# First-batch theta as float32 products, with the weights' two-part split moved beside the second attention

## The chip, the cores and the metric

The kernel runs on one core of a Trainium2 chip. The metric is the device time of one execution in microseconds. Three runs of the kernel before gave 557.42, 557.12 and 552.5 us, median 557.12 us. The profiled execution took 554.9 us, of which the span from the first to the last instruction is 553.1 us.

## The reference

The computation is a chain of three blocks over 4 batches of 576 positions with 512 channels.

- Windowed attention with 8 heads of 64 channels. Each position sees at most 32 keys, plain neighbours in heads 0 to 3 and every fourth position in heads 4 to 7. The result x has shape (4, 576, 512).
- A mixing block: theta = x @ w_theta, zr = x cos(theta), zi = x sin(theta), y = w_tok_r zr + w_tok_i zi over the positions, u = x + y, and x2 = u + relu(u @ w_ch).
- A gated block: h = relu(x2 @ w_in), its second half normalised and mixed over positions with w_spatial and b_spatial, multiplied with the first half, times w_out.

The weights arrive as float64 and are turned to float32 on the chip.

## The kernel before, in words

**Products in parts.** Outside the attention a float32 product is made of three products of type float32r (F32R): an operand a is split into a rounded part ah and a rest al, and a @ b is ah bh + al bh + ah bl. Three instructions per contraction block of 128, so twelve per tile where the contraction is 512. The attention's own products, and the transposes, are plain float32 (F32) instructions of TensorE (L252, L280, L294, L298, L372). A score product (L252) fills one half of the output's rows; two successive ones fill the two halves.

**Weights from float64.** `bits64` (L116) loads a piece of a weight, scales its high words on an engine (L130 on ScalarE or L132 on GpSimd) and puts the bits together in three VectorE instructions (L133 to L135) by way of one PSUM tile, c64. `split_weight` (L138) then copies the rounded part (L108, L110 or L112, by engine) and subtracts it for the rest (L146, GpSimd or VectorE). For w_theta (`w_theta_job`, L161, eight jobs: four blocks k of 128 rows, two halves c of 256 columns) copy and subtraction are both on GpSimd. The jobs are put between the score steps of the first batch's attention (L512 to L515), each tied behind the softmax of a step. Their loads stand in SP's queue ahead of those of w_tok.

**Theta.** `th_unit(b, t)` (L339) works on 128 positions (t = 0 to 3), or on the last 64 (t = 4). It scales x by 1/(2 pi) into the rounded part h (L352 on ScalarE in batch 0, L354 on VectorE later), makes the rest l (L355, VectorE), and issues the twelve products into one PSUM tile (L360). The result, in turns, is reduced to its fraction (L368 on ScalarE, L369 on VectorE), x is transposed on TensorE (L372), sine and cosine come from ScalarE (L377, L378, and L374 for the absolute value), VectorE multiplies them with the transposed x (L381, L388, L389), and the two results are split into zh (L110, L112 or L108) and zl (L332 on GpSimd).

**Order of the work.** Each engine works through its instructions in order. The program sets that order from generators that are run side by side (`spread`, L471, with rates), and a planner with its own estimate of times arranges what it emits. The first batch runs attention(0) with the w_theta jobs, then th_run(0) in the order t = 4, 0, 1, 2, 3 with the first half of w_tok beside it (L522), then tm_run(0) (the products with w_tok, L431 and L438) with attention(1) and the job list `j_tok1 + j_ch` beside it (L525 to L527), where j_ch are the four w_ch jobs. th_run(1) comes after (L528). Loads for the heads of attention(1) are tied behind the last load of the first half of w_tok (L234).

**Buffers.** ps_mm has 4 PSUM tiles, used by scores, theta and the w_tok products. The `stage` tiles of `bits64` are 4, the tiles xh and xl of theta 2 each.

Of the kernel before, what the change touches and what calls it, by code (L numbers as in the profile page):

```python
# [11 lines left out]
F32 = mybir.dt.float32  # L12
F32R = mybir.dt.float32r
BF16 = mybir.dt.bfloat16
U32 = mybir.dt.uint32
AF = mybir.ActivationFunctionType
ALU = mybir.AluOpType
# [5 lines left out]
DM = H * D  # L23
P = 128
# [12 lines left out]
INV2PI = float(np.float32(1.0 / (2.0 * math.pi)))  # L37
# [15 lines left out]
IN_ENG, SP_ENG, OUT_ENG = "vgg", "ag", "aga"  # L53
TOK_ENG = ("aga", "gv")
CH_ENG = "vga"
THETA_ENG = "gg"
Z_HI = ("v", "g")

K_MAIN = (0, 4, 1, 5, 2, 6, 3, 7)
# [4 lines left out]
def tile_block(ctx: ExitStack, tc: tile.TileContext, qT, kT, vw, eye_in, mask_in, eye_b_in, w_theta, w_tok, w_ch, w_in, w_sp, w_sph, b_sp, w_out, out):  # L64
    nc = tc.nc
    V, A, G, PE, SY = nc.vector, nc.scalar, nc.gpsimd, nc.tensor, nc.sync

    def f32(ap):
        return ap.bitcast(F32)
# [3 lines left out]
    ps_mm = ctx.enter_context(tc.tile_pool(name="ps_mm", bufs=4, space=PSUM))  # L73
# [18 lines left out]
    pz = tc.alloc_tile_pool(name="pz", bufs=1, side="left")  # L92
# [3 lines left out]
    pth = tc.alloc_tile_pool(name="pth", bufs=1, side="right")  # L96
    wth_h = pth.tile([P, 4, DM], F32R, name="wth_h")
    wth_l = pth.tile([P, 4, DM], F32R, name="wth_l")
# [7 lines left out]
    def copy(dst, src, eng):  # L106
        if eng == "a":
            A.copy(dst, src)  # L108
        elif eng == "v":
            V.tensor_copy(dst, src)  # L110
        else:
            G.tensor_scalar(dst, src, 1.0, 1.0, op0=ALU.mult, op1=ALU.mult)  # L112
# [3 lines left out]
    def bits64(src, n, eng, st=None):  # L116

        p = src.shape[0]  # L120
        if st is None:
            st = const.tile([P, 2 * CH], U32, tag="w64", name="w64", bufs=4)
        last_dma[0] = SY.dma_start(st[:p, :2 * n], src.bitcast(U32))
        w = st[:p, :2 * n].rearrange("p (n w) -> p n w", w=2)
        lw, hw = w[:, :, 0], w[:, :, 1]
        g = const.tile([P, CH], F32, tag="stage", name="w64g", bufs=4)[:p, :n]
        c = c64[:p, :n].bitcast(U32)
        gi = g.bitcast(U32)
        if eng == "a":
            A.mul(g, hw.bitcast(F32), 2.0**-112)  # L130
        else:
            G.tensor_scalar(g, hw.bitcast(F32), 2.0**-56, 2.0**-56, op0=ALU.mult, op1=ALU.mult)  # L132
        V.tensor_scalar(c, lw, 29, None, op0=ALU.logical_shift_right)  # L133
        V.scalar_tensor_tensor(c, gi, 3, c, op0=ALU.logical_shift_left, op1=ALU.bitwise_or)
        V.scalar_tensor_tensor(gi, gi, 0x80000000, c, op0=ALU.bitwise_and, op1=ALU.bitwise_or)  # L135
        return g

    def split_weight(src, hi, lo, eng_hi, eng_lo, eng_bits="g", st=None):  # L138
        n = hi.shape[-1]
        if src.dtype == F32:  # L140
            s = const.tile([P, CH], F32, tag="stage", name="stage", bufs=4)[:src.shape[0], :n]
            SY.dma_start(s, src)
        else:
            s = bits64(src, n, eng_bits, st)
        copy(hi, s, eng_hi)
        (G if eng_lo == "g" else V).tensor_tensor(lo, s, f32(hi), op=ALU.subtract)  # L146

    def halves(src, hi, lo, k, n, engs):

        for c in range(2):  # L150
            cs = slice(n // 2 * c, n // 2 * (c + 1))
            split_weight(src[:, k, cs], hi[:, k, cs], lo[:, k, cs], *engs)

    def stored(src, dst, k, cs, engs):
# [3 lines left out]
        split_weight(src[:, k, cs], t[:, 0], t[:, 1], *engs)  # L158
        SY.dma_start(f32(dst[:, k, :, cs]), f32(t))

    def w_theta_job(k, c):  # L161
        cs = slice(DM // 2 * c, DM // 2 * (c + 1))
        split_weight(w_theta[:, k, cs], wth_h[:, k, cs], wth_l[:, k, cs], *THETA_ENG, st=pz.tile([P, DM], U32, tag=f"z{'hl'[c]}{k}", name="wth64"))

    def w_tok_job(k, c):
        cs = slice(CH * c, CH * (c + 1))
# [4 lines left out]
    def w_ch_job(k):  # L171
        if not wch:
            wch.extend(p1.tile([P, 4, DM], F32R, tag=n, name=n) for n in ("wch_h", "wch_l"))
        halves(w_ch, *wch, k, DM, CH_ENG)
# [155 lines left out]
    def split(dst_h, dst_l, src, eh="a", el="g"):  # L330
        copy(dst_h, src, eh)
        return (G if el == "g" else V).tensor_tensor(dst_l, src, f32(dst_h), op=ALU.subtract)  # L332

    def ztile(k, bufs=1):
        h = pz.tile([P, DM], F32R, tag=f"zh{k}", name=f"zh{k}", bufs=bufs)
        l = pz.tile([P, DM], F32R, tag=f"zl{k}", name=f"zl{k}", bufs=bufs)
        return h, l

    def th_unit(b, t, pair=False):  # L339


        n = P if pair or t < 4 else HALF
        if pair:
            src = xs[b]
            V.tensor_copy(src[:, :, HALF:], x[b + 1][:, :, 4 * P:])
        else:
            src = x[b][:, :, P * t:P * t + n]
        h = pth.tile([P, 4, P], F32R, tag="xh", name="xh", bufs=2)[:, :, :n]
        l = pth.tile([P, 4, P], F32R, tag="xl", name="xl", bufs=2)[:, :, :n]

        if b == 0:
            A.mul(h, src, INV2PI)  # L352
        else:
            V.tensor_scalar(h, src, INV2PI, None, op0=ALU.mult)  # L354
        V.scalar_tensor_tensor(l, src, INV2PI, f32(h), op0=ALU.mult, op1=ALU.subtract)  # L355
        ps = ps_mm.tile([P, 512], F32, tag="mm", name="ps_th")[:n]
        i = 0
        for k in range(4):
            for lh, rh in ((h, wth_h), (l, wth_h), (h, wth_l)):
                PE.matmul(ps, lh[:, k, :], rh[:, k, :], start=(i == 0), stop=(i == 11))  # L360
                i += 1
        if b == 0 and t in (0, 1):
            if not t:
                spare.append(p1.tile([P, 4, DM], F32, tag="uh", name="spare"))
            ta, tb = (spare[0][:, 2 * t + i, :] for i in range(2))
        else:
            ta, tb = (pth.tile([P, DM], F32, tag=g, name=g, bufs=2)[:n] for g in ("ta", "tb"))
        A.activation(ta, ps, AF.Identity, bias=magic[:n, 0:1])  # L368
        V.scalar_tensor_tensor(ta, ta, MAGIC, ps, op0=ALU.subtract, op1=ALU.subtract)  # L369
        xn = ps_t.tile([P, 512], F32, tag="pt", name="ps_xn")[:n]  # L370
        for k in range(4):
            turned[b, t] = PE.transpose(xn[:, P * k:P * (k + 1)], src[:, k, :], ident)  # L372
        if b == 0:
            A.activation(tb, ta, AF.Abs)  # L374
        else:
            V.tensor_scalar(tb.bitcast(U32), ta.bitcast(U32), 0x7FFFFFFF, None, op0=ALU.bitwise_and)
        A.activation(ta, ta, AF.Sin, scale=-TURN)  # L377
        ia = A.activation(tb, tb, AF.Sin, scale=-TURN, bias=half_pi[:n, 0:1])  # L378
        if t < 4:
            for k, tt in ((t, tb), (4 + t, ta)):  # L380
                iv = V.tensor_tensor(tt, xn, tt, op=ALU.mult)  # L381
                zh[b, k], zl[b, k] = ztile(k)
                zlast[b] = ia, iv, split(zh[b, k], zl[b, k], tt, Z_HI[k // 4], "g")
        else:
            for i in range(2 if pair else 1):
                r_ = slice(HALF * i, HALF * (i + 1))
                zz = pth.tile([P, DM], F32, tag=("ta", "tb")[i], name="zz", bufs=2)
                V.tensor_tensor(zz[:HALF], xn[r_], tb[r_], op=ALU.mult)  # L388
                V.tensor_tensor(zz[HALF:], xn[r_], ta[r_], op=ALU.mult)  # L389
                zh[b + i, 8], zl[b + i, 8] = ztile(8, 2)  # L390
                split(zh[b + i, 8], zl[b + i, 8], zz, "a", "g")
# [9 lines left out]
    def th_shared(b):  # L401
        th_unit(b, 4, True)
        yield

    def th_run(b, ts):
        for t in ts:
            th_unit(b, t)
            yield
# [84 lines left out]
        for g in gens:  # L493
            yield from g

    j_ch = [lambda k=k: w_ch_job(k) for k in range(4)]

    H2 = DM // 2
    j_in = [lambda k=k, c=c: stored(w_in, win_d, k, slice(H2 * c, H2 * (c + 1)), IN_ENG) for c in (2, 3, 0, 1) for k in range(4)]
# [12 lines left out]
    for m, _ in enumerate(attention(0)):  # L512
        for i in range(8):
            if m == TH_FROM + TH_RATE * i // 10:
                behind(softmax[m], lambda: w_theta_job(i // 2, i % 2))  # L515
# [49 lines left out]
    for hf in (1, 0):  # L565
        cs = slice(DM * hf, DM * (hf + 1))
# [3 lines left out]
    n = 0  # L570
# [61 lines left out]
    gg = {}  # L632
# [212 lines left out]
```

## Time and profile before

| what | value |
|---|---|
| runs (us) | 557.42, 557.12, 552.5 |
| median | 557.12 us |
| profiled execution | 554.9 us |
| its span | 553.1 us, 11234 instructions |
| busy: TensorE products, weight loads | 531.0 us, 474.5 us |
| busy: VectorE, ScalarE, GpSimd | 320.3, 244.2, 262.9 us |
| mean granted TensorE clock | 0.997 of full speed |

Times are microseconds from the start of the span. PE is TensorE's products, PEld its weight loads, DVE is VectorE, ACT ScalarE, POOL GpSimd, SP the queue that issues most transfers. A product's recorded duration has the way through the array in it; how fast products follow each other is read from the starts.

### The profile page before, as it was taken

To read this page: it belongs to the slowest core of one execution; us is meant where nothing else is said; L and a number is where in the kernel's file an instruction comes from. 1 tells how busy PE (TensorE), PEld (TensorE's weight loads), DVE (VectorE), ACT (ScalarE), POOL (GpSimd) and SP (SyncE) were. 2 spreads that over 40 slices of the span, in tenths; PEclk is the share of its full clock that TensorE was granted. 3 is DMA by queue.
4 is the path that set the end of the run, shared out by engine and by line. 5 is a ranking of instruction groups with operands and counts; after the bars stand their busy time and mean duration, and the time that the engine had idled before them with its cause. 6 is when DMAs were issued, how large, how long until landed. Compare 5 with 4: busy or idle time off the path is not lost.

```text
span 553.1 us, 11234 instructions
## 1 busy us (share of the span) xinstructions
PE 531.0 (96%) x4148; PEld 474.5 (86%) x4148; DVE 320.3 (58%) x835; ACT 244.2 (44%) x717; POOL 262.9 (48%) x333
## 2 busy tenths in 40 slices
PE   5997999999999999988999999999999999999997
PEld 3665888989889989877889999899899889988996
DVE  2698998898787487632694139862702148253020
ACT  3869765635656254663452114542322233233221
POOL 3494994645984359641188336363202204322040
PEclk9999999999999999998999999999999999999999
DMA  8925766660588353770005978848015110002002
GB/s 203 300 93 156 191 180 189 182 198 35 162 235 232 95 175 120 230 228 25 1 1 155 370 250 286 265 131 289 20 58 172 58 38 1 1 1 77 0 1 96
DMA packets 50223, 76.07 MB, mean 138 GB/s; under 512 B 4084, under 2 KB 30968, under 8 KB 50168
## 3 DMA queue, kind: packets, MB, share of 16 engines
q1 hardware_dynamic: 49944, 75.17, 44.3%
q8 instruction: 33, 0.54, 0.4%
q10 hardware_dynamic: 224, 0.18, 0.1%
q14 instruction: 22, 0.18, 0.1%
HBM read 52.53 MB, written 22.81 MB: 136 GB/s over the span
## 4 chain that ended last, share of the span: by engine, by line
PE 52%; DMA 3%; POOL 1%; ACT 1%; issue 1%; DVE 1%; SPq 0%; ACTq 0%; POOLq 0%; DVEq 0%
PE ps_sp L719 9%; PE ps_hu L700 9%; PE ps_o L748 9%; PE ps_hv L655 9%; PE ps_y L438 7%; PE ps_r L457 4%; PE ps_th L360 1%; DMA wsp_d<-parts 1%; DMA win_d<-parts 1%; PE ps_sp L722 1%; PE ps_sp L721 1%; POOL zl L332 0%; POOL parts L146 0%; ACT parts L108 0%; DVE ta L381 0%
## 5 line engine op out<-in xcount | busy, mean ns | idle before, releaser
L438 PE MATMUL ps_y<-wtok_h,zh 128*128 128x288 f32 x270 | 82.1, 308 | 0.7 <-DVE sm L263 0.4
L438 PE MATMUL ps_y<-wtok_h,zl 128*128 128x288 f32 x270 | 81.0, 301 | 0.4 <-POOL zl L332 0.4
L438 PE MATMUL ps_y<-wtok_l,zh 128*128 128x288 f32 x270 | 79.8, 299 | 0.0
L332 POOL TENSOR_TENSOR gl<-hu,gh 128x288 fp32r<-128x288 f32 x32 | 26.0, 813 | 71.4 <-ACT gh L108 71.4
L438 PEld LDWEIGHTS ps_y<-wtok_h,zh 128*128 128x128 f32 x270 | 50.7, 189 | 3.2 <-DVE sm L263 0.9
L438 PEld LDWEIGHTS ps_y<-wtok_h,zl 128*128 128x128 f32 x270 | 51.2, 189 | 1.7 <-POOL zl L332 0.8
L723 DVE TENSOR_TENSOR hu<-ps_sp,hu 128x288 f32<-128x288 f32 x32 | 14.6, 456 | 63.5 <-PE ps_sp L722 63.5
L438 PEld LDWEIGHTS ps_y<-wtok_l,zh 128*128 128x128 f32 x270 | 50.7, 189 | 0.6
L332 POOL TENSOR_TENSOR vl<-hv,vh 128x512 fp32r<-128x512 f32 x16 | 20.9, 1308 | 58.1 <-ACT vh L108 53.1
L270 POOL TENSOR_TENSOR sm<-sm,l 128x288 f32<-128x288 f32 x48 | 32.0, 672 | 27.6 <-DVE l L269 14.7
L267 ACT ACTIVATE sm<-sm,m 128x96 f32<-128x96 f32 x108 | 39.2, 364 | 12.8 <-DVE m L264 6.7
L332 POOL TENSOR_TENSOR ul<-x,uh 128x288 fp32r<-128x288 f32 x32 | 26.7, 841 | 26.4 <-ACT uh L108 26.1
L719 PE MATMUL ps_sp<-wsp_h,vh 128*128 128x288 f32 x128 | 37.8, 295 | 0.0
L457 PE MATMUL ps_r<-uh,wch_h 128*128 128x288 f32 x128 | 37.6, 300 | 0.2 <-DVE x L441 0.2
L719 PE MATMUL ps_sp<-wsp_l,vh 128*128 128x288 f32 x128 | 37.8, 295 | 0.0
L719 PE MATMUL ps_sp<-wsp_h,vl 128*128 128x288 f32 x128 | 37.8, 295 | 0.0
L700 PE MATMUL ps_hu<-x2h,win_h 128*128 128x288 f32 x128 | 37.7, 294 | 0.0
L700 PE MATMUL ps_hu<-x2h,win_l 128*128 128x288 f32 x128 | 37.7, 294 | 0.0
L700 PE MATMUL ps_hu<-x2l,win_h 128*128 128x288 f32 x128 | 37.7, 294 | 0.0
L457 PE MATMUL ps_r<-uh,wch_l 128*128 128x288 f32 x128 | 37.5, 296 | 0.0
L441 DVE TENSOR_TENSOR x<-ps_y,x 128x288 f32<-128x288 f32 x40 | 17.6, 448 | 33.9 <-PE ps_y L438 33.8
L457 PE MATMUL ps_r<-ul,wch_h 128*128 128x288 f32 x128 | 36.7, 295 | 0.0
(182 smaller groups left out, 1577.7 us busy)
## 6 DMA issues: line engine op xcount, KB each, us to landing
x2d<-parts SPq DMA_DIRECT2D x32, 288.0 KB, 2.7
vt<-vw SPq DMA_DIRECT2D x16, 432.0 KB, 4.6
w<-w_tok SPq DMA_DIRECT2D x18, 288.0 KB, 4.7
x2h<-x2d SPq DMA_DIRECT2D x8, 576.0 KB, 7.8
x2l<-x2d SPq DMA_DIRECT2D x8, 576.0 KB, 8.3
kt<-kT SPq DMA_DIRECT2D x15, 304.0 KB, 4.2
w<-w_in SPq DMA_DIRECT2D x16, 256.0 KB, 3.3
win_d<-parts SPq DMA_DIRECT2D x16, 256.0 KB, 2.5
```

The lines of the kernel that those rows point to most:

```text
L267: ia = A.activation(sm[:, t, :], src[:, t, :], AF.Exp, bias=m_[:, t:t + 1], scale=scale, accum_out=l[:, t:t + 1])
L270: ig = G.tensor_tensor(sm, sm, l.unsqueeze(2).to_broadcast([P, 3, KW]), op=ALU.mult)
L332: return (G if el == "g" else V).tensor_tensor(dst_l, src, f32(dst_h), op=ALU.subtract)
L360: PE.matmul(ps, lh[:, k, :], rh[:, k, :], start=(i == 0), stop=(i == 11))
L438: PE.matmul(ps[:, :CH], lh[b, k][:, P * d:P * (d + 1)], rh[:, k, cs], start=(n == 0), stop=(n == 3 * len(ks) - 1))
L441: V.tensor_tensor(xv, ps[:, :CH], xv, op=ALU.add)
L457: PE.matmul(ps[:, :CH], lh[:, k, P * e:P * (e + 1)], rh[:, k, cs], start=(n == 0), stop=(n == 11))
L655: PE.matmul(ps, lh[:, k, ts_], rh[:, k, DM:], start=(n == 0), stop=(n == 11))
L700: PE.matmul(ps[:, :CH], lh[:, k, fs], rh[:, k, cs], start=(n == 0), stop=(n == 11))
L719: PE.matmul(ps[:, :CH], lh[b, k][:, fs], rh[:, k, cs], start=(n == 0), stop=False)
L723: V.tensor_tensor(t[:, f, cs], ps[:, :CH], t[:, f, cs], op=ALU.mult)
L748: PE.matmul(ps, lh[:, k, ts_], rh[:, k, cs], start=(n == 0), stop=(n == 11))
```

## The change

In the first batch theta is one F32 product per block k (four in all), of x as it is and a weight tile `wth[k]` that w_theta_job makes: the float64 piece turned to float32 and multiplied by 1/(2 pi) on GpSimd, in place of the rounded copy and the subtraction. The four tiles of 128x512 lie in the buffers of xh and xl. The rounded part and the rest of these scaled weights are made by four new jobs, `w_theta_split(k)`, one ScalarE copy and one GpSimd subtraction of 128x512 each, at the end of the list that runs beside attention(1). From the second batch on the twelve products stay; h is now a plain copy of x on VectorE and l a plain difference, as the factor is in the weights.

```diff
+    wth = []
     def w_theta_job(k, c):
         cs = slice(DM // 2 * c, DM // 2 * (c + 1))
-        split_weight(w_theta[:, k, cs], wth_h[:, k, cs], wth_l[:, k, cs], *THETA_ENG, st=pz.tile([P, DM], U32, tag=f"z{'hl'[c]}{k}", name="wth64"))
+        if not c:
+            wth.append(pth.tile([P, DM], F32, tag=("xh", "xl")[k % 2], name="wth", bufs=2))
+        g = bits64(w_theta[:, k, cs], DM // 2, "g", pz.tile([P, DM], U32, tag=f"z{'hl'[c]}{k}", name="wth64"))
+        G.tensor_scalar(wth[k][:, cs], g, INV2PI, 1.0, op0=ALU.mult, op1=ALU.mult)
+    def w_theta_split(k):
+        split(wth_h[:, k, :], wth_l[:, k, :], wth[k], "a", "g")
...
-        h = pth.tile([P, 4, P], F32R, tag="xh", name="xh", bufs=2)[:, :, :n]
-        l = pth.tile([P, 4, P], F32R, tag="xl", name="xl", bufs=2)[:, :, :n]
+        ps = ps_mm.tile([P, 512], F32, tag="mm", name="ps_th")[:n]
         if b == 0:
-            A.mul(h, src, INV2PI)
-        else:
-            V.tensor_scalar(h, src, INV2PI, None, op0=ALU.mult)
-        V.scalar_tensor_tensor(l, src, INV2PI, f32(h), op0=ALU.mult, op1=ALU.subtract)
-        ps = ps_mm.tile([P, 512], F32, tag="mm", name="ps_th")[:n]
-        i = 0
-        for k in range(4):
-            for lh, rh in ((h, wth_h), (l, wth_h), (h, wth_l)):
-                PE.matmul(ps, lh[:, k, :], rh[:, k, :], start=(i == 0), stop=(i == 11))
-                i += 1
+            for k in range(4):
+                PE.matmul(ps, src[:, k, :], wth[k], start=(k == 0), stop=(k == 3))
+        else:
+            h = pth.tile([P, 4, P], F32R, tag="xh", name="xh", bufs=2)[:, :, :n]
+            l = pth.tile([P, 4, P], F32R, tag="xl", name="xl", bufs=2)[:, :, :n]
+            V.tensor_copy(h, src)
+            V.tensor_tensor(l, src, f32(h), op=ALU.subtract)
+            i = 0
+            for k in range(4):
+                for lh, rh in ((h, wth_h), (l, wth_h), (h, wth_l)):
+                    PE.matmul(ps, lh[:, k, :], rh[:, k, :], start=(i == 0), stop=(i == 11))
+                    i += 1
...
-    j_ch = [lambda k=k: w_ch_job(k) for k in range(4)]
+    j_ch = [lambda k=k: w_ch_job(k) for k in range(4)] + [lambda k=k: w_theta_split(k) for k in range(4)]
```

## Rows read from the trace of the kernel before

**Rows 1.** Busy time by stretch: length, PE, PEld, DVE, ACT, POOL, clock, DMA.

```profile
23.90:33.85 9.95, 7.77 (x135) 5.76 (x131) 9.49 (x28) 6.95 (x29) 9.44 (x19) 1.00 0.66 244
33.85:56.06 22.21, 18.18 (x84) 12.85 (x83) 19.92 (x41) 18.66 (x39) 14.13 (x19) 1.00 0.43 120
56.06:70.30 14.24, 13.04 (x127) 11.33 (x125) 14.21 (x35) 9.78 (x30) 14.16 (x16) 1.00 0.70 176
70.30:112.00 41.70, 41.69 (x435) 36.51 (x436) 38.13 (x109) 24.85 (x93) 28.29 (x46) 1.00 0.64 187
```

**Rows 2.** The chain that ended last, in order of time: start, length, what.

```profile
226.34 4.37 DMA win_d<-parts
...
266.34 2.77 PE ps_th L360 x12
...
299.33 28.62 PE ps_y L438 x216
```

**Rows 3.** Waits of TensorE's products, 33 to 80 us: total, times, longest.

```profile
PE ps_th L360 <- ACT xh L352: 1.9, 2, 1.1
PE ps_th L360 <- DVE xl L355: 1.5, 2, 0.8
PE s L252 <- DVE sm L263: 1.2, 1, 1.2
```

**Rows 4.** Timeline of TensorE's products around the first batch's theta: start, length, what.

```profile
20.78 0.72 PE L252 MATMUL s<-kt,qz_2wch_l 128*64 128x96 f32 x12
...
34.51 1.20 PE L372 MATMUL ps_xn<-ident,x 128*128 128x128 f32 x9 [0.15 <-ACT x L307]
35.47 0.47 PE L360 MATMUL ps_th<-wth_h,xh 128*64 128x512 f32 x1
...
42.58 0.50 PE L360 MATMUL ps_th<-wth_h,xh 128*128 128x512 f32 x1 [1.07 <-ACT xh L352]
...
56.06 0.29 PE L431 MATMUL ps_y<-wtok_h,zl 128*128 128x288 f32 x1
```

**Rows 5.** Timeline of ScalarE and GpSimd where the first attention ends.

```profile
31.39 0.67 POOL L270 TENSOR_TENSOR sm<-sm,l 128x288 f32<-128x288 f32 x1 [0.24 <-DVE l L269]
...
34.34 0.46 ACT L310 COPY x<-ps_x 128x144 f32<-128x144 f32 x1
```

**Rows 6.** GpSimd's groups, 24 to 41 us: count, busy us, mean ns, idle before.

```profile
L146 POOL TENSOR_TENSOR wth_l<-w64g,wth_h 128x256 fp32r<-128x256 f32 x8 | 6.3, 789 | 0.2
L112 POOL TENSOR_SCALAR wth_h<-w64g 128x256 fp32r<-128x256 f32 x8 | 3.4, 428 | 0.0
```

**Rows 7.** Single lines: count, shortest/median/longest ns, first and last start.

```profile
L352 ACT ACTIVATE xh<-x x5: 420/617/627, 34.8 to 50.2; 128x512 fp32r<-128x512 f32 x4, 128x256 fp32r<-128x256 f32 x1
...
L108 ACT CAST zh<-zz x4: 611/624/625, 51.4 to 273.1; 128x512 fp32r<-128x512 f32 x4
...
L332 POOL TENSOR_TENSOR zl<-ta,zh x14: 1273/1308/1557, 63.8 to 298.8; 128x512 fp32r<-128x512 f32 x14
...
L354 DVE TENSOR_SCALAR xh<-x x13: 414/428/958, 110.7 to 275.5; 128x512 fp32r<-128x512 f32 x12, 128x256 fp32r<-128x256 f32 x1
```

**Rows 8.** VectorE's groups, 33.85 to 70.3 us, columns as in rows 6.

```profile
L355 DVE SCALAR_TENSOR_TENSOR xl<-x,xh 128x512 fp32r<-128x512 f32 x4 | 3.4, 847 | 0.0
L355 DVE SCALAR_TENSOR_TENSOR xl<-x,xh 128x256 fp32r<-128x256 f32 x1 | 0.6, 568 | 0.0
```

**Rows 9.** VectorE's small additions; one on the timeline, with GpSimd beside it.

```profile
L268 DVE TENSOR_SCALAR l<-l x48: 131/169/1256, 9.9 to 251.7; 128x3 f32<-128x3 f32 x48
...
66.76 1.26 DVE L268 TENSOR_SCALAR l<-l 128x3 f32<-128x3 f32 x1
...
66.58 1.41 POOL L332 TENSOR_TENSOR zl<-ta,zh 128x512 fp32r<-128x512 f32 x1
```

**Rows 10.** Timeline where the second batch's theta begins: GpSimd, TensorE.

```profile
115.22 0.73 POOL L146 TENSOR_TENSOR wch_l<-w64g,wch_h 128x256 fp32r<-128x256 f32 x1
...
119.48 0.39 PE L360 MATMUL ps_th<-wth_l,xh 128*64 128x512 f32 x1
```

More of the change, by code (lines that the diff above doesn't have):

```diff
@@ L55 @@
 CH_ENG = "vga"
-THETA_ENG = "gg"
 Z_HI = ("v", "g")
```

## The prediction

> **What bounds the kernel now.** I read the busy times first: TensorE is busy 531.0 of 553.1 us, so a change counts only where TensorE waits, or where its own work changes. Then the busy times by stretch around the change, to find those places. From 23.9 to 33.85 us, the end of the first attention, TensorE is idle for 9.95 - 7.77 = 2.2 us; from there to 56.06, which is the first batch's theta, for 4.0 us; to 70.3 for 1.2 us; and from 70.3 to 112 us for nothing [rows 1]. After 70 us TensorE is the bound, so what is gained before it moves everything behind it, and what is hidden beside attention(1) costs nothing as long as TensorE stays full there. Third, the chain that ended last: in its earliest part it has stores of weight parts, each 4 us, and later mostly TensorE [rows 2]. These stores are paced by jobs that start with their own stage, so I take it that they move with an earlier start. Last, the waits and the timeline of the theta stretch. TensorE waits there for h (1.9 us) and for l (1.5 us) [rows 3]. The last copy of x starts at 34.34 and ends at 34.8, the first theta product starts at 35.47, and the second unit pair at 42.58 waits 1.07 us for h [rows 4, 5].
>
> Busy time flatters this stretch, since a waiting product's record has its way through the array in it. By starts: twelve products take 2.77 us, 0.23 each [rows 2], nine transposes (1.20 - 0.28)/8 = 0.115 each [rows 4]. Five units are 5 x 2.77 = 13.9 us, twenty transposes 2.3, two more products 0.3: 16.5 us of issue in a stretch of 22.2. So 5.7 us are lost.
>
> **The change part by part.**
>
> *Products of the first batch.* Sixty F32R products go, twenty F32 ones come. What does an F32 product of 512 columns cost? The six score products of a step stand in the trace as twelve instructions [rows 4], so a product is two. Twenty are thus forty, eight per unit. No F32 product of 512 columns is in the trace, so I bound one instruction. Lower end: the pace of F32R, 0.23 us, which gives 8 x 0.23 = 1.84 us per unit, 0.93 less than now, over five units -4.7 us of TensorE. Upper end: F32 transposes of 128 columns at 0.115 us, or 0.90 ns per column, so 0.46 us, 3.68 per unit, +4.6 us in all. The score products pass 12 instructions in 0.72 us; the last record is some 0.25 of it. They are 96 columns wide, fill two different halves of the rows in turn, and if the halves run together five steps took 0.47 us, 0.98 ns per column. If they run one after the other, that is 0.43 ns per column. So this row alone fits both ends; the transposes, which use all rows, decide, and F32 without a transpose is the nearest to them in type. I take 0.45 us, 3.6 per unit, **+4.2 us** of TensorE work (5 x 0.83).
>
> The Trainium skill, "FP8 and Floating Point Precision", section TensorE Precision Notes, says that true FP32 takes four passes through the array. That speaks against the change: at four times 0.23 us a unit would take 3.7 us, an estimate, and the sum below would be 0.5 us worse. No row here shows an F32 product of this width.
>
> *Waits of these products.* h and l go: five ScalarE scalings, 2.9 us (four of 0.62 and one of 0.42) [rows 7], and five VectorE subtractions, 4.0 us [rows 8]. The first product can then start as the last x copy lands, 34.8 in place of 35.47, and products of blocks k = 0 to 2 need neither the last block of x nor of the weights. TensorE's work in the stretch becomes 16.5 + 4.2 = 20.7 us. If it runs without gaps the stretch ends 1.5 us earlier; I keep 0.4 us of gaps: **-1.1 us**. Some products of k = 0 and 1 may fall into the 2.2 us that TensorE idles before 33.85; the planner decides. Bounds 0 and -2.2, I take **-0.6 us**, nearer the lower end because x and the transposes' results come in the same stretch.
>
> *Behind it.* From 56.06 to 70.3 VectorE is busy 14.21 and GpSimd 14.16 of 14.24 us [rows 1], and TensorE waits 1.2 us for a masked score on VectorE [rows 3]. VectorE now arrives 4.0 us lighter, and the first unit's result, some 3.6 us after 34.8, is earlier than now, where two units run in turn until 41.3. That wait should go: **-1.0 us** of 1.2, bounds 0 and -1.2. What is late next is TensorE itself.
>
> *GpSimd in the first attention.* Eight copies (3.4 us) become eight multiplications of the same form and size; eight subtractions (6.3 us) go [rows 6]. GpSimd is full there (9.44 of 9.95 us), but the last softmax product at 31.39 waited for VectorE [rows 5], so the attention's end hardly moves. I take 0, bounds 0 and -1.4 (two subtractions that stand ahead of it). The w_theta loads keep their place in SP's queue, and the stage tiles come free a subtraction earlier, which lets the first w_tok pieces in; no queue gets a new transfer.
>
> *The new split jobs.* Four ScalarE copies of 0.62 and four GpSimd subtractions of 1.3 us: 2.5 and 5.2 us [rows 7]. From 70.3 to 112 ScalarE idles 16.9 and GpSimd 13.4 us [rows 1]; that is their cover, and their input is ready before 40 us. Without the cover: if all four stood behind the last subtraction for w_ch (ends 115.95) [rows 10], the last would end at 121.2 where theta of the second batch needs it at 119.48, 1.7 us late. I take 0.
>
> *Later batches.* h as a plain copy in place of a scaling of 0.43 us [rows 7], l as a plain difference of the same size: 0, bounds +-0.3.
>
> Sum: -1.1 - 0.6 - 1.0 = **-2.7 us**. Against the profiled execution, 554.9 - 2.7 = 552.2 us; that execution lies 2.2 us below the median of the runs, from which the sum gives 554.4. I predict between the two, **553 us**.
>
> **The rivals.**
>
> *Slower: TensorE's added work is not covered.* The gaps of the theta stretch could stand where they are, because in 33.85 to 56.06 VectorE is busy 19.92 and ScalarE 18.66 of 22.21 us [rows 1] with float64 pieces of w_tok that stay, and each engine works in order. Then the +4.2 us come on top and only the l wait (1.5 us) goes: 554.9 + 2.7 = 557.6. It decides if the last first-batch theta product ends later than 56.06. Against it: h and l are themselves what the longest of these waits name.
>
> *Slower by the copies on VectorE.* A VectorE addition of three columns took 1.26 us beside a GpSimd subtraction that began before it, against 0.17 as a rule [rows 9]. Four moved subtractions could each hold VectorE 1.1 us in a stretch where it has 3.6 us of slack: 4.4 - 3.6 = +0.8, so 553.0 in place of 552.2. The Trainium skill, "SBUF — State Buffer", section Who interferes with whom, states a shared port that one of the two engines holds for a whole instruction; the trace agrees with its 1.26 us. This is inside the forecast.
>
> *No change: the gain is taken back.* Between 226 and 250 us the chain is made of stores [rows 2]. If they kept their times, an earlier start would be waited away: 554.9.
>
> *Faster: F32 at F32R's pace.* TensorE's work falls by 4.7 us; the stretch then ends when ScalarE and VectorE do, which lose 2.9 and 4.0 us. With all of the l and h waits (3.4), the score wait (1.2) and 1.0 of the early idle: -5.6, 549.3.
>
> *The change does not do what it says.* The planner may run the splits long before attention(1), as their input is there: GpSimd idles 8.1 us in 33.85 to 56.06 [rows 1], so 5.2 us fit and the time is that of the forecast.
>
> **How the numbers follow.** Forecast (gain of 1 to 4.5 us) 0.50, with early splits in it; uncovered work 0.15; taken back 0.17; F32 at F32R's pace, or all bounds on the good side at once (-1.5 - 2.2 - 1.2 - 1.4 = -6.3), 0.18. The three runs shown spread over 4.9 us, which widens each case by 2 to 3 us. The range takes the good bound less the spread, 547, to the slower rival plus it, 560. A measurement of this kernel can tell about 1%, 5.5 us, from no change. Faster by that: the last case with most of its chance and some of the forecast's tail, 0.22. Slower by that: half of the first rival, 0.08. Within 1%: 0.70.
>
> **What would show it.** Right: eight theta instructions per unit, near 0.45 us apart; no wait of theta products for x's parts; the last of them ending at 54 to 55 us; TensorE full until 112 us; the split's subtractions before 117 us. Wrong: instructions 0.23 us apart; theta ending after 56; gaps where theta's results wait for VectorE; or a stretch around 250 us that has kept its place.

## The result, and the profile after

The changed kernel takes 560.19 us (median of 15 runs, 556.67 to 563.79), the kernel before 556.2 us on the same chip (15 runs, 552.5 to 559.12). The ratio is 1.0074, 95% interval [1.0053, 1.0095]: slower by 0.7%, some 4 us, where 553 us and a gain were forecast. The profiled execution took 560.11 us with a span of 558.3 us, 5.2 us more than that of before; TensorE's mean granted clock over it is 0.991 of full speed, 0.997 before.

The first view is the busy time by stretch, the same four as in [rows 1]; columns as there.

```profile
23.90:33.85 9.95, 7.22 (x70) 3.87 (x67) 8.06 (x26) 5.67 (x27) 7.44 (x15) 0.87 0.76 269
33.85:56.06 22.21, 22.06 (x129) 10.41 (x129) 15.28 (x34) 14.74 (x34) 11.27 (x16) 0.98 0.44 125
56.06:70.30 14.24, 11.05 (x82) 8.45 (x81) 13.38 (x27) 12.79 (x30) 11.24 (x12) 0.76 0.64 159
70.30:112.00 41.70, 41.70 (x422) 36.45 (x421) 36.30 (x100) 23.34 (x93) 26.89 (x43) 1.00 0.53 158
```

The theta stretch, which had 4.0 us of idle TensorE, is now full. But the stretch behind it idles 3.2 us in place of 1.2, TensorE starts 82 products there in place of 127, and its granted clock is 0.76 where it was 1.00. VectorE, the fullest engine of the theta stretch before, falls from 19.92 to 15.28 us: its work now comes later.

TensorE's timeline shows why (start, length, what; in brackets the idle time ahead and what ended it):

```profile
30.91 4.63 PE L361 MATMUL ps_th<-wth,x 128*64 128x512 f32 x6 [0.68 <-POOL wth L169]
35.48 0.33 PE L304 MATMUL ps_x<-pT,vt 96*64 96x64 f32 x2
35.74 1.12 PE L361 MATMUL ps_th<-wth,x 128*128 128x512 f32 x2
...
38.49 3.80 PE L361 MATMUL ps_th<-wth,x 128*64 128x512 f32 x8
42.13 0.82 PE L290 MATMUL pt<-ident,sm 128*96 128x128 f32 x6
...
43.04 3.80 PE L361 MATMUL ps_th<-wth,x 128*64 128x512 f32 x8
46.77 0.85 PE L304 MATMUL ps_x<-pT,vt 96*64 96x64 f32 x21
...
52.52 4.46 PE L361 MATMUL ps_th<-wth,x 128*128 128x512 f32 x10
57.73 0.63 PE L382 MATMUL ps_xn<-ident,x 128*128 128x128 f32 x4 [0.75 <-DVE zz L399]
...
59.75 0.53 PE L441 MATMUL ps_y<-wtok_h,zh 128*128 128x288 f32 x2 [1.40 <-ACT zh L107]
...
61.35 0.29 PE L441 MATMUL ps_y<-wtok_l,zh 128*128 128x288 f32 x1
61.48 0.29 PE L441 MATMUL ps_y<-wtok_h,zl 128*128 128x288 f32 x1
...
63.11 0.61 PE L441 MATMUL ps_y<-wtok_h,zl 128*128 128x288 f32 x1 [0.84 <-POOL zl L342]
63.52 0.44 PE L441 MATMUL ps_y<-wtok_l,zh 128*128 128x288 f32 x1
63.76 0.44 PE L441 MATMUL ps_y<-wtok_h,zl 128*128 128x288 f32 x1
```

Theta (L361) starts at 30.91, and 6 + 2 + 8 + 8 = 24 of its 40 instructions stand in TensorE's queue ahead of the last head pair's values products (L304, 21 from 46.77). Then, behind theta, three waits of 0.75, 1.40 and 0.84 us for what the other engines make of theta, and products that follow each other at 0.24 us (63.52, 63.76) where they took 0.13 (61.35, 61.48): the clock has fallen to its lower level. A clock of 0.76 over 14.24 us is half speed for 2 x 0.24 x 14.24 = 6.8 us, so up to 3.4 us of work lost. In the same way 0.87 and 0.98 in the two stretches ahead are 2.6 + 0.9 = 3.5 us at half speed, up to 1.7 us of work.

ScalarE's timeline: the last copy of x, and the first and last of the five operations (L378) that round a unit's result.

```profile
48.46 0.48 ACT L320 COPY x<-ps_x 128x144 f32<-128x144 f32 x1
...
50.22 0.68 ACT L378 ACTIVATE ta<-ps_th,magic 64x512 f32<-64x512 f32 x1 [0.71 <-PE ps_th L361]
...
61.46 0.68 ACT L378 ACTIVATE ta<-ps_th,magic 128x512 f32<-128x512 f32 x1
```

x is whole at 48.9 us; before, at 34.8 [rows 5]. The 24 early instructions are three units' worth, and yet no unit's result was read before 50.22: they are parts of several units. In the kernel before, ScalarE rounds the first result at 41.3 us (first and last start stand behind the three durations):

```profile
L368 ACT ACTIVATE ta<-ps_th,magic x3: 670/683/687, 41.3 to 56.8; 128x512 f32<-128x512 f32 x2, 64x512 f32<-64x512 f32 x1
```

One more landmark serves for all versions, the first product with w_ch's parts: after, then before.

```profile
L467 PE MATMUL ps_r<-uh,wch_h x128: 290/295/402, 115.3 to 345.8; 128*128 128x288 f32 x128
```

```profile
L457 PE MATMUL ps_r<-uh,wch_h x128: 292/294/406, 108.5 to 340.6; 128*128 128x288 f32 x128
```

It is 6.8 us late at 115.3, which covers the 5.2 us of the span. About 1.0 us of it was there before any changed instruction: the first long run of values products starts at 18.72 in place of 17.75 us, behind a load of queries. The two stretches at the lower clock can be up to 5.1 us of it in this one execution; whether they are what makes the kernel slower is answered at the end of the experiments.

GpSimd's timeline shows the first of the four split subtractions; the last starts at 43.16. They did not wait for the second attention.

```profile
33.06 1.27 POOL L342 TENSOR_TENSOR wth_l<-wth,wth_h 128x512 fp32r<-128x512 f32 x1
```

### The profile page after: what moved, and what is told of

The parts are those of the page before. It is cut to its first block, busy times and chain, and to the rows that moved or that the text cites. A ratio compares the mean times of both kernels' runs of the same rounds, so it can differ in the third digit from the quotient of the medians.

```text
span 558.3 us, 11183 instructions
## 1 busy us (share of the span) xinstructions
PE 537.4 (96%) x4128; PEld 471.2 (84%) x4128; DVE 322.8 (58%) x831; ACT 245.1 (44%) x717; POOL 259.9 (47%) x329
## 4 chain that ended last, share of the span: by engine, by line
PE 69%; DVE 8%; DMA 7%; ACT 5%; POOL 5%; issue 4%; SPq 1%; POOLq 0%; ACTq 0%; DVEq 0%
PE ps_y L448 15%; PE ps_sp L729 9%; PE ps_hu L710 9%; PE ps_o L758 9%; PE ps_hv L665 9%; PE ps_r L467 5%; PE s L262 3%; PE pt L290 2%; PE ps_th L361 2%; POOL zl L342 2%; DMA wth<-w_theta 2%; DMA win_d<-parts 2%; PE ps_th L370 1%; DMA kt<-kT 1%; PE ps_y L441 1%
## 5 line engine op out<-in xcount | busy, mean ns | idle before, releaser
L448 PE MATMUL ps_y<-wtok_h,zh 128*128 128x288 f32 x270 | 80.7, 304 | 1.5 <-DVE sm L273 0.5
L467 PE MATMUL ps_r<-ul,wch_h 128*128 128x288 f32 x128 | 36.6, 295 | 0.0
```

Of the source, the lines that this page charges most:

```text
L448: PE.matmul(ps[:, :CH], lh[b, k][:, P * d:P * (d + 1)], rh[:, k, cs], start=(n == 0), stop=(n == 3 * len(ks) - 1))
L467: PE.matmul(ps[:, :CH], lh[:, k, P * e:P * (e + 1)], rh[:, k, cs], start=(n == 0), stop=(n == 11))
```

## The experiments

The theory after these readings: float32 products need no h and l and, block by block, not all of x, so the planner puts them ahead of the attention that makes the rest of x, and block by block over the units, so that all units finish together. Rivals: the float32 products cost more than forecast; the splits, run early, are in the way; the fallen clock is the loss. Each run is timed beside the kernel before, whose median was 556.29 to 556.5 us.

**Theta's order in the queue.** Two runs, one edit each: the first ties all first-batch theta products behind the last values product, the second holds the splits behind the softmax of step 17, which is the sixth of the second attention.

```
+            with tc.issue_after(values[11].ins):
                 for k in range(4):
                     PE.matmul(ps, src[:, k, :], wth[k], ...)
```

> The changed kernel with the first batch's theta products queued on TensorE behind the last value product of the first attention; nothing else is touched. Order theory (the loss comes from theta products that the planner put into TensorE's queue ahead of the attention's values, which moved the end of x from 34.8 to 48.9 us): x is complete near 36 us, theta ends before 57, and the time falls by 4 us or more against the changed kernel, to 553 to 557. Cost theory (the loss is the F32 products' extra 4.2 us of TensorE work, wherever it stands): 559 to 561, as the changed kernel. Split theory (the loss comes from the four splits that GpSimd and ScalarE do during the first attention): 559 to 561, since the splits stay there.

Measured: 557.79 us (12 runs), ratio 1.0037 [1.001, 1.0064].

```
+    j_ch = ... + [lambda k=k: behind(softmax[17], lambda: w_theta_split(k)) for k in range(4)]
```

> The changed kernel with the four split jobs queued behind the sixth softmax of the second attention on ScalarE and GpSimd, so that they cannot run in the first attention. Split theory: 555 to 557, the loss is gone. Order theory and cost theory: 559 to 561, and x is complete near 49 us as in the changed kernel.

Measured: 561.49 us (8 runs), ratio 1.0091 [1.0058, 1.0124]. The tie alone brings back about half of the loss, 2.4 us in the medians where 4 or more were expected, and the two intervals overlap a little. Holding the splits alone brings nothing (they ran from 87.5 us), and its stretch from 56.06 has the clock of 0.76 again; the tied kernel's, second here, has 1.00.

```profile
56.06:70.30 14.24, 11.81 (x88) 10.07 (x89) 13.35 (x27) 11.10 (x28) 12.48 (x13) 0.76 0.26 72
```

```profile
56.06:70.30 14.24, 11.31 (x117) 9.71 (x114) 13.55 (x28) 13.28 (x27) 12.93 (x13) 1.00 0.24 69
```

With the tie x is early (last copy at 36.67), but the five roundings come at 48.61 to 59.15: the products still go block by block over the units, as far as the late results show it, and TensorE waits for what follows (timeline of the tied kernel):

```profile
38.86 5.32 PE L362 MATMUL ps_th<-wth,x 128*128 128x512 f32 x12
...
50.76 5.32 PE L362 MATMUL ps_th<-wth,x 128*128 128x512 f32 x12
...
57.26 0.53 PE L442 MATMUL ps_y<-wtok_h,zh 128*128 128x288 f32 x2 [0.75 <-ACT zh L107]
...
60.69 0.41 PE L442 MATMUL ps_y<-wtok_h,zl 128*128 128x288 f32 x1 [0.90 <-POOL zl L342]
```

**Units in sequence, splits held.** Each unit's products are issued behind the last product of the unit before.

```
+            with tc.issue_after((th_last[-1] if th_last else values[11]).ins):
                 for k in range(4):
+                    mm = PE.matmul(ps, src[:, k, :], wth[k], ...)
+            th_last.append(mm)
+    (splits held as above)
```

> Theta products behind the attention's last value product, the five units one after the other in TensorE's queue, splits held as in the second run. Order theory: first unit's result near 39 us, last theta product at 54 to 56 us, 551 to 555. Cost theory: 559 to 561. If the order costs something but the price of F32 is a term too: between 555 and 558.

Measured: 551.52 us (12 runs), ratio 0.9924 [0.9897, 0.9951]: faster than both kernels. In its timeline theta is one run behind the attention's end, and the first results are used at 54.71:

```profile
34.80 0.52 PE L308 MATMUL ps_x<-pT,vt 96*64 96x64 f32 x12
35.15 1.88 PE L364 MATMUL ps_th<-wth,x 128*64 128x512 f32 x4
...
39.52 15.01 PE L364 MATMUL ps_th<-wth,x 128*64 128x512 f32 x34
...
54.71 0.38 PE L445 MATMUL ps_y<-wtok_h,zh 128*128 128x288 f32 x1
...
62.84 0.40 PE L445 MATMUL ps_y<-wtok_h,zl 128*128 128x288 f32 x1 [0.40 <-POOL zl L342]
```

Its windows, in the columns of [rows 1]:

```profile
33.85:56.06 22.21, 22.21 (x106) 10.96 (x105) 19.58 (x41) 17.75 (x38) 11.49 (x17) 1.00 0.49 142
56.06:70.30 14.24, 13.59 (x122) 11.79 (x121) 13.76 (x34) 9.16 (x29) 13.88 (x17) 1.00 0.65 179
```

The theta stretch is full, VectorE has its work back in it, the next stretch idles 0.65 us, and the clock is 1.00 in both.

**The price of a product.** The same kernel with the products of block k = 1 left out of the first batch's theta (15 products in place of 20; its output lacks that part of the sum).

```
-                for k in range(4):
+                for k in (0, 2, 3):
```

> As the run with the units in sequence, but the product of block k = 1 is left out of the first batch's theta, so that its theta holds fifteen F32 products in place of twenty: about as much TensorE time as the sixty F32R products of the kernel before. Cost theory: 4.5 us less than with all four, as TensorE has 5 x 0.9 us less to do in a stretch that it bounds. Order theory with other engines as the bound of the stretch: less than 2 us less.

Measured: 555.25 us (12 runs), ratio 0.9966 [0.9937, 0.9996]: five products fewer bring no gain, and the median is even 3.7 us above the full version's 551.52, with intervals that overlap a little. The profiled spans are 549.1 and 549.0 us. In the stage the products show: theta's first and last instructions start 14.5 us apart (33.4 and 47.9) in place of 18.7, and the first w_ch product comes at 103.3 in place of 107.6 us. Of these 4.3 us, 1.7 were there when x was whole (34.9 against 36.6 us), and thus not by the products.

```profile
L471 PE MATMUL ps_r<-uh,wch_h x128: 290/295/401, 103.3 to 336.5; 128*128 128x288 f32 x128
```

```profile
L471 PE MATMUL ps_r<-uh,wch_h x128: 290/294/402, 107.6 to 336.5; 128*128 128x288 f32 x128
```

Both rows end at 336.5: the 4.3 us are given back by then. Between 33 and 110 us TensorE waits 3.3 us for loads of queries, a wait that the full version doesn't have (total, times, longest):

```profile
PE s L262 <- DMA qz<-qT: 3.3, 2, 2.4
```

The price of the products isn't what made the changed kernel slow, and time gained in the first stage isn't sure to reach the end.

**The sequence taken apart.** First the changed kernel with the sequence and nothing else; then sequence and tie with the splits free; then the kernel before, its twelve F32R products per unit in the same sequence and with the same tie.

```
+            with tc.issue_after(th_last[-1].ins) if th_last else nullcontext():
```

> The changed kernel with one edit: the first batch's five theta units one after the other in TensorE's queue; not tied behind the attention, splits not held. Interleaving theory (half of the loss is that the planner takes block k of all units before the next block, so that all five results come together at the end): first result near 40 us, 551 to 555, as the run with everything in order. If what counts is the theta products ahead of the attention's values alone: two of the first unit's products still stand there, 557 to 560.

Measured: 555.36 us (12 runs), ratio 0.9998 [0.997, 1.0026], just above the 551 to 555 expected. In the medians the sequence alone takes the whole loss away. Only four of theta's instructions (at 28.84, 29.32, 34.16 and 34.59 us) still stand ahead of the last values products, so this edit does two things at once: it ends the mixing of the units, and it takes 20 of the 24 early instructions out of the attention. The first result is rounded at 40.3 us:

```profile
L382 ACT ACTIVATE ta<-ps_th,magic x3: 670/678/689, 40.3 to 54.1; 128x512 f32<-128x512 f32 x2, 64x512 f32<-64x512 f32 x1
```

```
     (tie and sequence as above)
+    j_ch = ... + [lambda k=k: w_theta_split(k) for k in range(4)]
```

> The kernel with products behind the attention and units in sequence (551.5 us with the splits held), but the four splits free to run in the first attention again. Split theory in a weaker form: the splits cost 1 us or more, 553 to 555. If they cost nothing where they stand: 550.5 to 552.5.

Measured: 555.36 us (12 runs), ratio 0.9986 [0.9962, 1.0011]. In the medians the tie adds nothing once the units are in sequence (but see the clocks below); holding the splits, which was worth nothing with the units mixed, is now worth the difference from 0.9986 to 0.9924, about 3.5 us. I had read the splits as free.

```
+        with tc.issue_after((th_last[-1] if th_last else values[11]).ins) if b == 0 else nullcontext():
             (the twelve F32R products of before)
```

> The kernel before, twelve F32R products per unit and all, with nothing changed but the order: its five first-batch units one after the other behind the attention. If the gain of the ordered version comes from the order and not from the F32 products: 550 to 553, as much as there or more. If the gain needs what the change took off VectorE, ScalarE and GpSimd (h, l, the weights' subtractions): 555 to 557, as the kernel before.

Measured: 560.59 us (6 runs), ratio 1.0088 [1.0062, 1.0115]. The sequence is not a gain by itself: with the products of before, sequence and tie cost some 5 us, with float32 products they save. Neither expectation had that loss. In its profile theta products still wait for l and for weight parts (1.1 and 0.7 us); that no other unit may go ahead meanwhile may be the reason, but isn't shown.

**An earlier first unit.** Sequence and held splits, but the first unit tied only behind the third head pair.

```
+            with tc.issue_after((th_last[-1] if th_last else values[8]).ins), (tc.issue_after(values[11].ins) if th_last else nullcontext()):
```

> The ordered version with splits held, but the first unit's products allowed ahead of the last head pair's values (behind those of the third pair), the other four units behind the attention. If TensorE's idle time in the attention can be used without harm: 1 us less than the ordered version, 549.5 to 551.5. If every product ahead of the values delays x: x complete about 1 us later and 551.5 to 553.5.

Measured: 553.68 us (12 runs), ratio 0.9949 [0.9931, 0.9967]: not better than behind the attention, with intervals that overlap; x is whole at 36.9 us.

**Which part of the splits costs.** Three more beside each other: ScalarE's copies free and only GpSimd's subtractions held; both named behind a values product; and the sequence with held splits once more.

```
+        copy(wth_h[:, k, :], wth[k], "a")
+        behind(softmax[17], lambda: G.tensor_tensor(wth_l[:, k, :], wth[k], f32(wth_h[:, k, :]), op=ALU.subtract))
```

> The kernel with units in sequence and splits held (551.5 us), with ScalarE's four split copies free again and only GpSimd's four subtractions held behind the softmax of step 17. Theory: what the early splits cost is a subtraction of 1.27 us that stands on GpSimd ahead of the last softmax product (32.37 us with free splits, 31.28 with held ones, from equal starts): 551 to 553 us, and that product follows no subtraction. Rival, ScalarE's copies are what costs: 555 to 556, as with free splits. Rival, the later order alone makes the difference: anywhere between, with a first w_ch product at 106 to 108 us.

Measured: 551.35 us (12 runs), ratio 0.9918 [0.9887, 0.995], as with all held: the early subtractions on GpSimd are what costs, the copies are not. They ran from 81.7 us.

```
+    j_ch = ... + [lambda k=k: behind([values[11]], lambda: w_theta_split(k)) for k in range(4)]
```

> The same with copies and subtractions both held, but only behind the last values product of the first attention, so that they may run in the theta stretch. Theory (they cost where they stand ahead of the attention's end): 551 to 553 us. Rival, they cost by filling GpSimd before 70 us, wherever: 555 us. Rival, the later order: anywhere between.

Measured: 554.54 us (12 runs), ratio 0.9968 [0.9945, 0.999]. The edit did not do what I meant: an order behind a TensorE product binds TensorE's queue alone, and the first subtraction still ran at 31.71. So it is a second kernel with free splits, and it can't tell a place ahead of the attention's end from one behind it. Its profile shows the mechanism; GpSimd, then TensorE:

```profile
31.71 1.27 POOL L342 TENSOR_TENSOR wth_l<-wth,wth_h 128x512 fp32r<-128x512 f32 x1
32.94 0.66 POOL L280 TENSOR_TENSOR sm<-sm,l 128x288 f32<-128x288 f32 x1
33.69 0.89 POOL L169 TENSOR_SCALAR wth<-w64g 128x256 f32<-128x256 f32 x2
...
33.66 0.87 PE L290 MATMUL pt<-ident,sm 128*96 128x128 f32 x3 [0.49 <-POOL sm L280]
```

The subtraction stands directly ahead of the last softmax product, for whose result TensorE's transposes then wait. In the kernel with the early first unit, where the splits are held and GpSimd starts on w_theta 0.05 us from the other (23.77 and 23.82 us), the same product goes at 31.28:

```profile
31.28 0.66 POOL L280 TENSOR_TENSOR sm<-sm,l 128x288 f32<-128x288 f32 x1
```

In the kernel with sequence, tie and free splits, which starts on w_theta at 23.63 us, it goes at 32.37, again directly behind a subtraction:

```profile
31.13 1.27 POOL L342 TENSOR_TENSOR wth_l<-wth,wth_h 128x512 fp32r<-128x512 f32 x1
32.37 0.66 POOL L280 TENSOR_TENSOR sm<-sm,l 128x288 f32<-128x288 f32 x1
```

> The kernel with units in sequence and splits held once more, beside the two others. If the order is what makes it fast: 550.5 to 552.5 us, and a ratio to the kernel before of 0.990 to 0.995. If its first time was a lucky one: 554 to 556. Its profile started 2.3 us late, behind a load of queries; if that load's time changes from run to run, the first w_ch product now comes 1 to 3 us before 107.6 us; if it belongs to the kernel, at 107.6 again.

Measured: 552.49 us (12 runs), ratio 0.9927 [0.9898, 0.9957]: the gain holds. Its profile started late again (long values run at 19.64 us; 20.06 in the first profile). In both TensorE waited for a load of queries (2.30 us in the first, 1.76 in this one) and then ran at the lower clock until some 19.3 us. The kernel with fifteen products has neither (17.16 us). But its span is 554.2 us against 549.0, the w_ch product comes at 109.6 against 107.6, and from there to the start of the dense last stage (the first ps_hv product) it took 225.6 us against 222.4. Two profiles of one kernel thus differ by 5 us. This execution was the longest of its twelve and had a mean clock of 0.988, the first profile 0.997. All versions lie between 222.4 and 229.8 us in that part, so I draw nothing from such differences in single profiles; the sizes come from the medians.

**The clock, execution by execution.** Every execution beside these runs has its mean granted clock on record, and within a kernel the time follows it: the 11 executions of the kernel before with 0.997 average 554.4 us, the 24 with 0.988 average 556.9 us. One slope for all kernels, fitted to the 226 executions on record with a clock, is 3.6 us per 0.01 of clock. The last column is an estimate from that fit, good to about 0.4 us.

| kernel | executions | mean clock | us at a clock of 0.994, estimate |
|---|---|---|---|
| before | 89 | 0.990 | 555.2 |
| changed | 15 | 0.993 | 559.8 |
| tie alone | 12 | 0.993 | 557.9 |
| splits held alone | 8 | 0.991 | 560.4 |
| sequence alone | 12 | 0.997 | 557.2 |
| sequence and tie, splits free; the second with splits named behind a values product | 12, 12 | 0.993, 0.994 | 555.5, 554.6 |
| sequence, tie, held splits; first and second time | 12, 12 | 0.996, 0.995 | 552.8, 552.7 |
| the same with fifteen products | 12 | 0.990 | 553.3 |

The changed kernel's executions had no lower clock than those of before, and at equal clock it is still 4.6 us slower: the clock is not the loss. At equal clock the tie takes 1.9 us off and the sequence 2.6, and together they take off 4.3 to 5.2. So part of what the sequence alone gained came with a higher clock, and the tie is worth something beside it. Held splits are worth 2 to 3 us, and five products fewer nothing. An order with fewer waits may itself raise the clock; the runs don't show that apart, and the medians stay the measure of each edit.

## Why the prediction was wrong

**The step that failed** is the one that let products of blocks 0 and 1 "fall into the 2.2 us that TensorE idles before 33.85; the planner decides", with bounds of 0 and -2.2, together with "the attention's end hardly moves". I gave the planner's choice no bound on the side of a loss. It did not fill a gap: it put 24 instructions ahead of work that the rest waited for, and mixed the units, so that the first result was read at 50.2 in place of 41.3 us. x came 14 us later. The runs show the price: with the units in sequence and nothing else changed the ratio goes from 1.0074 to 0.9998, 4.2 us of 556; with the tie alone to 1.0037. At equal clock the tie, which ends the early place, takes off 1.9 of 4.6 us, and the sequence beside it, which ends the mixing, another 2.4 to 3.3: each has its share. The fallen clock is not the cause of the loss: the profiles of the changed kernel and of the one with only the splits held have 0.76 from 56.06 to 70.3 us where those with the tie or the sequence have 1.00, but several of the latter have 0.66 to 0.82 in the stretch before 33.85, and over all executions the changed kernel's clock is no lower than that of before.

**The rival with that result was there for another reason.** "Slower: TensorE's added work is not covered" gave 557.6 us and was to decide if theta ended after 56.06. It did, its last instruction starting at 56.4, but not since gaps stayed with full work on top: the stretch has no gaps, and half of its work stood in the wrong place. With the order set right theta ends at 53.9 + 0.6 = 54.5 us, inside the forecast's 54 to 55. And the 0.70 for a change within 1% came true by luck: it stood on a small gain, and what was measured is a small loss with another cause.

**The splits at no cost.** My price was 0, and a rival let them run early at no cost as well, because GpSimd idles 8.1 us in the theta stretch. They ran early, and with the order right they cost 2 to 4 us: 551.5, 552.5 and 551.35 us with the subtractions held, 555.4, 555.4 and 554.5 with them free. The idle time was a sum over the stretch; at 31 to 34 us GpSimd was full, and the last softmax product stood behind a subtraction. The place ahead of the attention's end explains some 1.1 us of that (32.37 against 31.28 between two kernels whose starts on w_theta differ by 0.14 us; a subtraction lasts 1.27); where the rest goes stays open.

**What held.** Two instructions per product: 40 records for 20 products. At full clock the run of 34 in the sequenced kernel takes 15.01 us with a last record of 0.59, so (15.01 - 0.59)/33 = 0.437 us each; I had taken 0.45 out of 0.23 to 0.46. The term is +3.6 us (a unit of 8 x 0.437 = 3.50 in place of 2.77, five times) where I had +4.2. The Trainium skill, "FP8 and Floating Point Precision", section TensorE Precision Notes, has four passes for true FP32; at 0.23 us that would be 0.92 us a product, an estimate, and the trace has 0.87, near it. That rule did speak for the right side of my bounds, and it isn't why the kernel lost. The waits for h and l are gone. The masked-score wait of 1.2 us is 0.24 in the sequenced kernel. Held splits ran from 80.2 us there, beside the second attention, and TensorE stayed full from 70.3 to 112 us (41.70 of 41.70), as forecast. With both orders set, the gain is 0.8% or 4 us in the medians, where the forecast's parts sum to 2.7.

**The premise that a gain before 70 us moves everything behind it** held only in part: leaving out five products shortened theta by 4.2 us and moved the end by nothing, in the profiles and at equal clock. The rival "taken back" names that, with the stores near 226 to 250 us as its reason. The run shows 3.3 us of it as waits for loads of queries before 110 us; whether stores take the rest isn't shown.

## What to carry to other kernels

When a change takes away an input that held an instruction back, ask what the planner will do with its freedom: in an in-order queue an instruction that is ready earlier may stand ahead of work that more depends on, so that step needs a bound on the losing side. Set the order by hand for the first try (whole units in turn, behind the stage that feeds them) and judge the arithmetic after that. Idle time summed over a stretch is no cover for an instruction that lands just ahead of a critical one.

## What was not expected of the hardware

TensorE's granted clock fell to its lower level (1.2 of 2.4 GHz) at about 61.9 us, behind waits of only 0.75 and 1.40 us from 57 to 60 us (the one of 0.84 came when it had fallen), and was back at about 68.7; products of 288 columns meanwhile followed each other at 0.24 us instead of 0.13. The kernel with the tie had waits of 0.75, 0.57 and 0.90 us there and kept a clock of 1.00.

The changed kernel had been at the lower level once before, from about 31.3 to 34.5 us: theta's first six instructions took 4.63 us from 30.91, where eight took 3.80 from 38.49. Shortest, median and longest record of a theta instruction are 591, 592 and 1222 ns.

```profile
L361 PE MATMUL ps_th<-wth,x x40: 591/592/1222, 30.9 to 56.4; 128*128 128x512 f32 x32, 128*64 128x512 f32 x8
```

Much of the spread between executions of one kernel goes with the clock: 0.01 of mean clock went with some 3.6 us, about as much as the larger edits moved.
